# Moving the last 2 KB of every wo row onto seven chosen DMA engines by a software-issued side load

## Chip, cores, metric

One core of one Trainium2 chip. The metric is device microseconds of one execution. The profile's page counts 16 DMA engines for the core (its queue rows are shares of 16 engines' span). The kernel before takes 196.09 us (median of 3 runs, 195.96 to 196.11).

## The reference, cut to what matters

One decoding step for a batch of 4: attention of 32 query heads over the last 4096 positions of 8 key/value heads, then the output projection with `wo`, mixed with a small gated feed-forward block.

```
q = x @ wq                      # heads 32 x 128
p = softmax(q @ k.T * Dh**-0.5)  # k, v: last 4096 positions, 64 MB together
o = p @ v
a = o.reshape(B, 32 * 128) @ wo # wo is 4096 x 512 bf16: 4 MB, the last thing loaded
out = g * a + (1 - g) * ffn(x)
```

About 81 MB must come from memory once. Everything else hides behind that, except the work that follows the last bytes of `wo`.

## The kernel before: the parts in question

`Wo` is a tile of 128 partitions with 32 KB of `wo` each, cut into 64 units of 512 B per partition. It arrives in five pieces. All loads are issued by the sync engine (hardware queue), the last piece in three row blocks of 123, 3 and 2 rows.

```python
WO_PIECES = ((0, 34), (34, 52), (52, 60), (60, 63), (63, 64))   # units of 512 B
LOW3 = (0, 123, 126, 128)                                       # row blocks of the last piece
...
            elif k == "wo":
                lo, hi = WO_PIECES[it[1]]
                wo = A_wo.rearrange("(p i) c -> p (i c)", i=32)
                for n, r in enumerate(wo_rows(it[1])):           # 128 rows, or the LOW3 blocks
                    load(("WO", it[1], n), f"d_wo{it[1]}", Wo[r, OW * lo:OW * hi], wo[r, OW * lo:OW * hi], waits=w)
...
        def WO(p):                                               # tensor engine, one matmul a unit
            lo, hi = WO_PIECES[p]
            w = [("WO", p, n) for n in range(len(wo_rows(p)))] + [("E", "OQ")]
            for x in range(lo, hi):
                i, j = x // OUTT, x % OUTT
                mm(banks[ACC][OR * j:OR * j + 4, 0:OW], oq[:, i, :], Wo[:, OW * x:OW * x + OW], False, i == 31, ...)
```

Loads go out in the order wq, x, gate_w, the K and V sets, W_gate, W_up, last V, W_down, wo pieces. The slot of `wo` is free once the value product of set 6 is done, at 170.9 us.

## Time and profile before

| | before |
|---|---|
| time | 196.09 us |
| span of the profiled execution | 194.8 us |
| mean DMA rate | 416 GB/s |
| last landing of wo | 192.60 us |
| engines that land late (put down to instruction fetches below) | 6 of 16 |

The page's slice rows (40 slices of 4.9 us: busy share of the DMA engines in tenths, and GB/s) and its queue rows (packets, MB, share of 16 engines' span):

```profile
DMA  6999999999999999999999999999999999999992
GB/s 215 431 432 431 437 437 431 431 427 451 431 437 437 446 427 424 431 437 431 431 431 431 427 424 437 444 437 431 431 431 421 431 395 427 470 431 384 425 404 90
q1 hardware_dynamic: 3610, 81.01, 97.3%
q8 instruction: 5, 0.08, 0.2%
q14 instruction: 1, 0.01, 0.0%
```

From the second slice to the last but one the engines are busy 90% or more (9 tenths): the kernel is bound by its loads. The five 16 KB packets of q8, of the kind "instruction", are instruction fetches; they took 1.02 to 1.07 us each.

The end of the chain that ended last (start us, us, what):

```profile
171.74 20.41 DMA slots<-in_A_wo_dram
192.16 0.04 issue
192.20 0.87 PE bank L320 x12
193.07 0.02 issue
193.09 0.42 DVE osum L577
```

The tensor engine waits for `wo`. The twelve matmuls after 192.20 are the third piece's last eight units and the four units of the last two pieces; among them is one more wait, for the landing at 192.60.

Two stretches (window us, busy time of the engines, granted clock, DMA share, GB/s):

```profile
176.00:180.00 4.00, 1.51 (x8) 0.84 (x10) 0.00 (x0) 0.00 (x0) 0.00 (x0) 0.74 0.98 417
180.00:184.00 4.00, 4.00 (x38) 2.09 (x35) 0.00 (x0) 0.44 (x1) 0.00 (x0) 0.83 1.00 422
```

The page does not show the engines one by one. The trace does, in a way: it has sixteen landings for each of these loads, read here as one for each engine. Sorted landings (us) of the third wo piece (60 units of each row are then there), and of the fourth (63 units):

```
before, 60 units: 190.20 190.25 190.32 190.33 190.37 190.38 190.40 190.49 190.50 190.71 | 191.45 191.93 191.94 191.95 192.04 192.16
before, 63 units: 190.70 190.75 190.83 190.84 190.89 190.89 190.90 190.98 191.09 191.23 | 191.88 192.35 192.37 192.40 192.47 192.60
```

Ten engines are early, six late by 1.0 to 1.8 us, counted from the median of the ten. The gaps appear one by one, after each of the five 16 KB fetches and the one 8 KB fetch at 63.3 us (0.33 us): one late landing of sixteen after the first fetch, three after the third, six after the sixth. That a late engine is one that carried a fetch is inferred from this: no record names an engine. The unevenness is what the old last piece, and the change, try to use: give work to early engines. The three row blocks of the old last piece have eight landings together (191.87 to 192.39; three earlier updates of their semaphore, up to 184.90, precede the piece's first packet at 190.30), not sixteen each.

### The profile page before, as it was taken

Reading aid. Unit: us, or ns where it says so; the run is one execution under the profiler, and the core shown is the slowest. Engines: PE = TensorE matmul, PEld = TensorE weight load, DVE = VectorE, ACT = ScalarE, POOL = GpSimd, SP = SyncE. Lnnn points to the kernel's source line nnn. Section 1 sums busy time; section 2 is a strip of 40 time slices with the busy share of each in tenths; the row PEclk is TensorE's granted clock in tenths of the full one; section 3 lists DMA queues with packets and bytes.
Section 4 is the critical chain, followed back from the end, with each engine's and each line's share of the span. In section 5 each row is a group of like instructions: output and inputs, shape, how many; then the busy total and the mean of one; then the engine's idle time right before and its main releaser. Section 6 shows DMA issues by size and latency. Waiting matters only on the chain.

```text
span 194.8 us, 1734 instructions
## 1 busy us (share of the span) xinstructions
PE 120.6 (62%) x723; PEld 50.6 (26%) x723; DVE 124.1 (64%) x153; ACT 27.5 (14%) x34; POOL 9.5 (5%) x25
## 2 busy tenths in 40 slices
PE   0209279474943894686468943894586466743974
PEld 0003123121411341242112411341142122311562
DVE  6103769999399809980998199819981998370010
ACT  2213000040130013001300130013001300420100
POOL 7830000000000000000000000000000000000000
PEclk9999958999999797899876999697999889997899
DMA  6999999999999999999999999999999999999992
GB/s 215 431 432 431 437 437 431 431 427 451 431 437 437 446 427 424 431 437 431 431 431 431 427 424 437 444 437 431 431 431 421 431 395 427 470 431 384 425 404 90
DMA packets 3616, 81.10 MB, mean 416 GB/s; under 512 B 401, under 2 KB 666, under 8 KB 794
## 3 DMA queue, kind: packets, MB, share of 16 engines
q1 hardware_dynamic: 3610, 81.01, 97.3%
q8 instruction: 5, 0.08, 0.2%
q14 instruction: 1, 0.01, 0.0%
HBM read 81.01 MB, written 0.00 MB: 416 GB/s over the span
## 4 chain that ended last, share of the span: by engine, by line
DMA 54%; DVE 31%; PE 9%; issue 4%; SPq 0%; ACT 0%
DMA slots<-in_A_k_cache_dram 38%; DVE kt L491 21%; DMA slots<-in_A_wo_dram 10%; PE bank L320 7%; DMA xsb<-in_A_x_dram 6%; DVE sc L527 5%; DVE qblk L517 1%; PE bank L324 1%; DVE pT L542 1%; DVE rd L531 1%; SPq L256 0%; DVE negmax L537 0%; ACT gwB L600 0%; DVE osum L577 0%; DVE mx L527 0%
## 5 line engine op out<-in xcount | busy, mean ns | idle before, releaser
L491 DVE STREAM_TRANSPOSE kt<-slots 128x2048 f32<-128x2048 f32 x32 | 73.7, 2305 | 28.1 <-DMA slots<-in_A_k_cache_dram 28.0
L320 PE MATMUL bank<-kt,qblk 128*128 128x512 bf16 x256 | 72.1, 434 | 27.9 <-DVE kt L491 27.9
L320 PEld LDWEIGHTS bank<-kt,qblk 128*128 128x128 bf16 x256 | 25.2, 107 | 69.7 <-DVE kt L491 36.0
L320 PE MATMUL bank<-slots,pT 128*64 128x512 bf16 x256 | 32.3, 410 | 5.7 <-DMA slots<-in_A_v_cache_dram 5.7
L619 ACT ACTIVATE pe<-sc,negmax 128x2048 bf16<-128x2048 bf16 x8 | 16.0, 2002 | 60.1 <-DVE negmax L537 60.1
L527 DVE CUSTOM_DVE_ANT_0 sc<-bank,maskf 128x512 bf16<-128x512 f32 x32 | 21.0, 658 | 3.8 <-PE bank L320 3.7
L320 PEld LDWEIGHTS bank<-slots,pT 128*64 128x64 bf16 x256 | 15.1, 118 | 23.2 <-issue 13.4
L542 DVE STREAM_TRANSPOSE pT<-pe 128x2048 bf16<-128x2048 bf16 x8 | 18.5, 2312 | 2.2 <-ACT pe L619 2.2
L604 ACT ACTIVATE osb<-bank 128x512 bf16<-128x512 f32 x8 | 4.8, 597 | 81.5 <-PE bank L320 81.5
L320 PE MATMUL bank<-rd,grpb 128*128 128x32 bf16 x8 | 1.6, 194 | 22.1 <-DVE rd L531 22.1
L555 DVE TENSOR_TENSOR oq<-bank,recip 64x128 bf16<-64x128 f32 x2 | 0.9, 434 | 12.3 <-PE bank L320 12.2
L320 PEld LDWEIGHTS bank<-rd,grpb 128*128 128x128 bf16 x8 | 0.8, 98 | 25.7 <-DVE rd L531 25.7
L495 DVE COPY xT<-bank 128x20 bf16<-128x20 bf16 x1 | 0.2, 171 | 8.0 <-PE bank L324 8.0
L320 PE MATMUL bank<-slots,oq 128*4 128x256 bf16 x64 | 4.0, 272 | 2.0 <-DMA slots<-in_A_wo_dram 2.0
L320 PE MATMUL bank<-slots,xT 128*4 128x512 bf16 (+1 forms) x64 | 5.0, 467 | 0.0
L320 PE MATMUL bank<-maskr,maskl 128*128 128x512 bf16 x1 | 0.6, 609 | 5.9 <-POOL maskr L296 5.9
L517 DVE TENSOR_SCALAR qblk<-bank 32x64 uint32<-32x64 uint32 x16 | 2.9, 215 | 2.1 <-PE bank L324 2.1
L324 PE MATMUL bank<-identb,xsb 5*128 5x5 bf16 x4 | 0.3, 168 | 5.7 <-DMA xsb<-in_A_x_dram 5.7
L577 DVE CAST osum<-bank 4x256 bf16<-4x256 f32 x1 | 0.4, 418 | 5.2 <-PE bank L320 5.2
L320 PEld LDWEIGHTS bank<-slots,oq 128*4 128x4 bf16 x64 | 2.5, 84 | 3.5 <-DMA slots<-in_A_wo_dram 2.9
L296 POOL TENSOR_SCALAR_AFFINE_SELECT fold<-fold 128x256 bf16<-128x256 bf16 x8 | 3.3, 417 | 1.1
L486 DVE MEMSET qblk<- 128x2304 uint32 x1 | 2.0, 1978 | 1.3 <-PEq L644 1.3
(59 smaller groups left out, 40.3 us busy)
## 6 DMA issues: line engine op xcount, KB each, us to landing
slots<-in_A_k_cache_dram SPq DMA_DIRECT2D x8, 4096.0 KB, 25.1
slots<-in_A_v_cache_dram SPq DMA_DIRECT2D x8, 4096.0 KB, 30.5
slots<-in_A_wq_dram SPq DMA_DIRECT2D x1, 4096.0 KB, 12.4
slots<-in_A_wo_dram SPq DMA_DIRECT2D x1, 2176.0 KB, 17.1
slots<-in_B_W_gate_dram SPq DMA_DIRECT2D x1, 1792.0 KB, 19.7
slots<-in_B_W_up_dram SPq DMA_DIRECT2D x1, 1792.0 KB, 23.6
slots<-in_B_W_down_dram SPq DMA_DIRECT2D x1, 1792.0 KB, 18.5
slots<-in_A_wo_dram SPq DMA_DIRECT2D x1, 1152.0 KB, 19.5
```

Of the source, the lines that this page charges most:

```text
L296: op(lambda: e.affine_select(dst, src, pattern, cmp, fill, base=base, channel_multiplier=mult), ev)
L320: E.op(lambda: t.matmul(out_, lhsT, rhs, start=start, stop=stop, tile_position=pos, skip_group_check=True), ev=ev, waits=waits)
L324: E.op(lambda: t.transpose(out_, in_, idn), ev=ev, waits=waits)
L486: E.op(lambda: v.memset(qblk[:, :, :, :, :].rearrange("p s h c e -> p (s h c e)"), 0.0), ev=("QZ",))
L491: E.op(lambda: v.transpose(kt[:, f, :].bitcast(FP32), slot("k", s)[:, 4096 * f:4096 * f + 4096].bitcast(FP32)), ev=("E", "KT", s, f), waits=w)
L517: E.op(lambda dst=dst, r=r, g=g: v.tensor_scalar(dst, src[r, g, 0:B, :, :], 0, None, op0=ALU.bitwise_or), ev=("E",) + keys[1] if (q, g) == ...
L527: E.op(lambda: v.tensor_tensor_reduce(sc[:, 512 * f:512 * f + 512], banks[scb(key)], R["maskf"][:, :], 1.0, -3.0e38, ALU.add, ALU.max, mx4 ...
L531: E.op(lambda: v.tensor_tensor(rd32[:, :, :], bc(R["own8"][:, :].unsqueeze(2), 2, 4), bc(mx4[:, :].unsqueeze(1), 1, 8), ALU.mult), ev=("MA ...
L542: E.op(lambda: v.transpose(pT[:, s % 2, :], pe[:, :]), ev=("E", "PT", s), waits=[("EXP", s)] + ([("PV", s - 2)] if s >= 2 else []))
L555: E.op(lambda g=g, r=r: v.tensor_tensor(oq[r, :, :].rearrange("p i b -> p b i"), banks[tr(key)][0:64, 128 * g:128 * g + 128].rearrange("p ...
L604: E.op(lambda: a.activation(osb[:, s, :], ob(s), ACTF.Copy), ev=("NORM", s), waits=[("PV", s)])
L619: E.op(lambda: a.activation(pe[:, :], sc[:, :], ACTF.Exp, bias=negmax[:, s % 2:s % 2 + 1], scale=SCALE, accum_out=rowsum[:, s:s + 1]), ev= ...
```

## The change

Intent: let the six late engines stop at unit 60, and bring units 60 to 63 (2 KB a row) as a side load on engines that are early. 119 of its rows go out by GpSimd's software descriptors, after a tiny "turn" transfer to shift which engines they use; 9 rows go by the sync queue. The side load is issued as soon as the slot is free and multiplied first. Core of the diff:

```diff
-WO_PIECES = ((0, 34), (34, 52), (52, 60), (60, 63), (63, 64))
-LOW3 = (0, 123, 126, 128)
+WO_PIECES = ((0, 32), (32, 48), (48, 56), (56, 60))
+SIDE = (60, 64)
+SIDE_ROWS = (0, 119, 124, 128)
...
+    sb("turn", [12, 2, 8], BF16)
...
+                if it[1] == 0:
+                    for n in (1, 2):
+                        load(("SIDE", n), "d_side_hw", *side(n), waits=w)
+                load(("WO", it[1]), f"d_wo{it[1]}", Wo[:, OW * lo:OW * hi], wo_all[:, OW * lo:OW * hi], waits=w)
... (GpSimd)
+        E.op(lambda: e.dma_start(R["turn"][:, :, :], gate_w[0:384].rearrange("(p t c) -> p t c", p=12, t=2)[:, :, 0:8]), ev=("TURN",),
+             ctr="d_turn")
+        E.op(lambda: e.dma_start(*side(0), max_dma_last_dim=1024), ev=("SIDE", 0), waits=[("TURN",)] + slot_wait[("wo", 0)],
+             ctr="d_side")
... (tensor engine: WO(None), the side units, comes before WO(0))
```

More of the change, by code (lines that the diff above doesn't have):

```diff
@@ L155, in _order @@
     o += [("SC", s, 3), ("SW", s), ("PV", s - 1), ("PT", s), ("RS", 1), ("GU",), ("PV", s), ("FFN",), ("OQ",)]
-    return o + [("WO", p) for p in range(len(WO_PIECES))]
+    return o + [("WO", None)] + [("WO", p) for p in range(len(WO_PIECES))]
 def _dma_order():
@@ L240, in sc_free, with side @@
         return [("E",) + sck[n]] if n >= 0 else [("INIT",)]
-    def wo_rows(p):
-        return [slice(a, b) for a, b in zip(LOW3, LOW3[1:])] if p == len(WO_PIECES) - 1 else [slice(0, 128)]
+    wo_all = A_wo.rearrange("(p i) c -> p (i c)", i=32)
+    def side(n):
+        r, c = slice(SIDE_ROWS[n], SIDE_ROWS[n + 1]), slice(OW * SIDE[0], OW * SIDE[1])
+        return Wo[r, c], wo_all[r, c]
     def set_of(s):
@@ L275, in sync @@
                 lo, hi = WO_PIECES[it[1]]
-                wo = A_wo.rearrange("(p i) c -> p (i c)", i=32)
-                for n, r in enumerate(wo_rows(it[1])):
-                    load(("WO", it[1], n), f"d_wo{it[1]}", Wo[r, OW * lo:OW * hi], wo[r, OW * lo:OW * hi], waits=w)
+                if it[1] == 0:
+                    for n in (1, 2):
+                        load(("SIDE", n), "d_side_hw", *side(n), waits=w)
+                load(("WO", it[1]), f"d_wo{it[1]}", Wo[:, OW * lo:OW * hi], wo_all[:, OW * lo:OW * hi], waits=w)
             else:
@@ L424, in WO @@
         def WO(p):
-            lo, hi = WO_PIECES[p]
-            w = [("WO", p, n) for n in range(len(wo_rows(p)))] + [("E", "OQ")]
+            lo, hi = SIDE if p is None else WO_PIECES[p]
+            w = [("SIDE", n) for n in range(3)] + [("E", "OQ")] if p is None else [("WO", p)]
             for x in range(lo, hi):
                 i, j = x // OUTT, x % OUTT
-                mm(banks[ACC][OR * j:OR * j + 4, 0:OW], oq[:, i, :], Wo[:, OW * x:OW * x + OW], False, i == 31,
+                mm(banks[ACC][OR * j:OR * j + 4, 0:OW], oq[:, i, :], Wo[:, OW * x:OW * x + OW], False, i == WO_PIECES[-1][1] // OUTT - 1,
                    ev=("WOP", p) if x == hi - 1 else None, waits=w if x == lo else (), pos=(0, OR * j))
@@ L623, in FIN @@
             E.op(lambda: a.activation(osum[:, 0:OW], banks[ACC][0:4, 0:OW], ACTF.Copy), ev=("OSUM", 0),
-                 waits=[("WOP", len(WO_PIECES) - 2)])
+                 waits=[("WOP", len(WO_PIECES) - 1)])
         fns = dict(ECONST=ECONST, GWB=GWB, EQ=EQ, GE=GE, RELU=RELU, EXP=EXP, NORM=NORM, FIN=FIN)
```

## The prediction

> **What bounds the kernel.** The transfers. In the page's slice rows the DMA share is 9 tenths in every slice from the second to the last but one, at about 431 GB/s; PE is busy 62%, DVE 64%. In the chain of waits the last long piece is the wo load (20.41 us, to 192.16); after it come only PE x12 (0.87 us) and the final copy (0.42 us). So the time is set by when the slowest of the 16 DMA engines finishes its share.
>
> **Engines are uneven.** The trace's landings[...] of wo's first piece come in two groups: ten at 186.11 to 186.63, six at 187.23 to 188.01. The packet records explain it: five 16 KB instruction fetches (about 1.05 us each[...]) and one 8 KB fetch fell on six engines. These six stay 0.8 to 1.6 us behind. The third piece (60 of 64 units of 512 B per row) lands by 192.16, the 3-unit piece by 192.60, and the tensor engine's last four multiplications start at 192.64.[...]
>
> **What the change does.** The common part shrinks from 63 to 60 units, so every slow engine loses 8 packets of 1536 B (65 ns each in the trace): 0.52 us. The last four units become a side load: 119 rows of 2 KB in a GpSimd-issued transfer, 9 rows on the sync queue[...].[...]
>
> **Costs.** Each chosen engine gets 17 rows as 34 packets of 1 KB at about 46 ns (the x rows' packets): an estimate of 1.5 us, plus 0.1 to 0.17 us of sync-issued rows[...]. Fast engines land their 60th unit at 190.2 to 190.7, so the chosen ones should now land at 191.7 to 192.3: level with the slow ones at about 192.15. The side load can start when the slot frees (170.9); interleaved with V, W_down and wo it delays fast engines there by up to 1.5 us, which hides behind the slow ones.[...] Its four units are multiplied first, from about 188. PE keeps 54 ns per unit.
>
> **Critical path.** Last landing 192.60 -> about 192.2, then four multiplications (0.4 us), copy 0.42 us, store unchanged. Gain about 0.4 us of 196.09, 0.2%. Prediction 195.70 us, range 195.35 to 196.15. Faster by over 2%: 0.005; within 2%: 0.98; slower by over 2%: 0.015.
>
> **What would show it.** Last wo landing 192.0 to 192.3 with all 16 engines within 0.5 us; 119x2 packets of 1 KB on a second queue, finished before 188; final PE group starting at about 192.2, idle before it ended by the wo load; copy at about 192.6; V's last landing moved by under 0.2 us.
>
> **What would make it wrong.** The 119 rows go to all 16 engines, or to engines that carry the instruction fetches: then the slowest engine gains nothing or loses up to 1.5 us. Instruction fetches move to other engines. Software descriptors prove slower than the 46 ns packets[...]. V lands late enough that PE, with 0.3 us of slack, becomes the limit.

The sum: 190.2 to 190.7 plus 1.5 us, and 0.1 us or so for the sync queue's rows, is 191.7 to 192.3; the last landing then goes from 192.60 to about 192.2, and 0.4 us off 196.09 is 195.7. The cost of "turn" (put at under 0.1 us) was no term of it. The 17 rows for each chosen engine are 119 / 7, and the seven was an assumption.

## The result

| | before | after |
|---|---|---|
| time, median | 196.05 us (195.96 to 196.11, 4 runs) | 198.59 us (198.21 to 198.80, 4 runs) |
| span of the profiled execution | 194.8 us | 197.2 us |
| last landing of wo | 192.60 us | 194.98 us |
| last landing of V / W_down | 178.35 / 182.65 us | 179.25 / 186.04 us |

The ratio is 1.0128 (95%: 1.0110 to 1.0146). A ratio here is the mean time of one kernel's fast runs over the mean of the other's in the same rounds, so not quite the ratio of the medians. The change lost 2.5 us; a gain of 0.4 us was predicted.

The same page rows after:

```profile
DMA  6999999999999999999999999999999999999991
GB/s 219 439 453 445 452 439 425 425 422 425 425 425 425 420 432 429 439 445 439 445 439 425 422 425 432 432 425 425 425 425 422 435 408 441 438 397 323 388 391 61
q1 hardware_dynamic: 3492, 80.77, 96.7%
q0 software_dynamic: 192, 0.25, 0.4%
q8 instruction: 5, 0.08, 0.2%
q14 instruction: 1, 0.01, 0.0%
```

The engines are as busy as before, but one slice (177.5 to 182.4 us) moves 323 GB/s where the kernel before moved 384 in the same slice and 431 and 425 in those beside it. "Busy" is the time packets were under way; slow packets look busy. The same two windows as before show it closer:

```profile
176.00:180.00 4.00, 0.61 (x4) 0.42 (x6) 0.00 (x0) 0.00 (x0) 0.00 (x0) 0.70 1.00 321
180.00:184.00 4.00, 4.00 (x21) 1.89 (x18) 0.00 (x0) 0.00 (x0) 0.00 (x0) 0.50 1.01 332
```

Same DMA share within 0.02, a fifth to a quarter less data. The issue on GpSimd and the end of the kernel, from the timeline (start us, us, engine, line, operation, tiles):

```profile
12.29 0.72 POOL L321 DMA_DIRECT2D turn<-in_gate_w_dram  x1 [0.19 <-issue]
171.64 0.97 POOL L323 DMA_DIRECT2D slots<-in_A_wo_dram  x1 [158.63 <-PE bank L330]
```

```profile
172.51 21.84 DMA slots<-in_A_wo_dram
194.35 0.04 issue
194.40 0.60 PE bank L330 x8
195.00 0.03 issue
195.03 0.40 PE bank L330 x4
195.43 0.02 issue
195.45 0.42 DVE osum L587
```

The last lines are the end of the chain after. Its form is the predicted one, a last landing, four multiplications (0.40 us), a copy (0.42 us), but it begins at 194.98 in place of 192.2.

Two facts of the trace say where the time went. First, the packet records: the software packets ran from 176.0 (4.4 us after their issue began at 171.64) to 184.8 us, and in that time the ordinary packets of all engines took longer. Mean duration of packets that started between 176 and 182 us (a packet of 14336 B is one row of `W_down`):

```
before: 14336 B packets 539 ns            (128 packets)
after:  14336 B packets 716 ns            (106 packets), software 4096 B packets 180 ns
```

The long packets stand everywhere: before, every one of the 128 packets took less than 560 ns; after, every one of the 106 took more than 600 ns, though the side rows, by the count of their packets (56 of 4096 B, 7 of 2048 B: 8 + 1 seven times), were on seven engines only. Second, the landings of the 60th unit of each row:

```
after, 60 units: 192.24 192.25 192.27 192.28 192.47 | 193.35 193.36 193.45 193.59 193.65 193.66 193.69 193.83 194.00 | 194.89 194.98
```

Even the five earliest engines land 2.0 us later than the five earliest of before (means 192.30 and 190.29). Nine engines follow, then two, 0.9 us behind the rest. The counts fit a simple reading, which is inferred and not recorded: seven engines with software side rows and six with a fetch, two of them with both, leave five with neither. In numbers: predicted last landing 192.2; fourteen engines done at 194.00 (1.8 us more; the five earliest lost as much); last two at 194.98 (1.0 us more).

### The profile page after: what moved, and what is told of

Same layout as the page of the kernel before. It is cut to its first block, busy times and chain, and to the rows that moved or that the text cites. A ratio compares the mean times of both kernels' runs of the same rounds, so it can differ in the third digit from the quotient of the medians.

```text
span 197.2 us, 1736 instructions
## 1 busy us (share of the span) xinstructions
PE 122.8 (62%) x723; PEld 51.7 (26%) x723; DVE 124.2 (63%) x153; ACT 27.5 (14%) x34; POOL 11.2 (6%) x27
## 4 chain that ended last, share of the span: by engine, by line
DMA 54%; DVE 30%; PE 9%; issue 5%; SPq 1%; ACT 0%
DMA slots<-in_A_k_cache_dram 37%; DVE kt L501 21%; DMA slots<-in_A_wo_dram 11%; PE bank L330 8%; DMA xsb<-in_gate_w_dram 6%; DVE sc L537 5%; PE bank L334 2%; DVE qblk L527 1%; DVE pT L552 1%; SPq L261 1%; DVE rd L541 1%; DVE negmax L547 0%; ACT gwB L610 0%; DVE osum L587 0%; DVE mx L537 0%
## 5 line engine op out<-in xcount | busy, mean ns | idle before, releaser
L330 PE MATMUL bank<-kt,qblk 128*128 128x512 bf16 x256 | 73.6, 440 | 26.4 <-DVE kt L501 26.4
L330 PEld LDWEIGHTS bank<-kt,qblk 128*128 128x128 bf16 x256 | 25.7, 109 | 69.6 <-DVE kt L501 34.1
L323 POOL DMA_DIRECT2D slots<-in_A_wo_dram x1 | 1.0, 972 | 158.6 <-PE bank L330 158.6
```

Source lines behind the costliest of these rows:

```text
L323: E.op(lambda: e.dma_start(*side(0), max_dma_last_dim=1024), ev=("SIDE", 0), waits=[("TURN",)] + slot_wait[("wo", 0)], ctr="d_side")
L330: E.op(lambda: t.matmul(out_, lhsT, rhs, start=start, stop=stop, tile_position=pos, skip_group_check=True), ev=ev, waits=waits)
```

## The experiments

A ring is here a DMA queue of the profile: q0 holds the software's transfers, q1 those of the sync engine, q10 those of the scalar engine. A turn is a change from one ring to another.

Theories at the start: A, every turn between the software ring and the hardware ring costs all engines time. B, two of the seven chosen engines also carry an instruction fetch. C, the bytes of the side load slow everybody.

### e1_single: one software packet per engine

```diff
-e.dma_start(*side(0), max_dma_last_dim=1024)
+e.dma_start(*side(0), max_dma_last_dim=1024, single_packet=True)
```

> The changed kernel with the software side load packed into one packet per engine (34 descriptors) in place of nine. Theory A, each turn between the software ring and the hardware ring costs every engine about 0.18 us and lengthens the hardware packets: with one turn the W_down packets of 14336 B go back from 710 ns to about 540 ns, the five fastest engines land wo at about 190.8 in place of 192.3, and the time falls to about 197.0 us; what is left over the kernel before (about 0.9 us) is theory B, side rows on two engines that carry instruction fetches. Rival C, the 238 KB that software descriptors move[...] slow everyone: unchanged, 198.5 us and 710 ns.

Measured: 198.49 us (198.34 to 198.82), ratio 1.0123. The option did nothing: the trace has the same 56 packets of 4096 B and 7 of 2048 B. So the run tests no theory. It is a repeat of the changed kernel, and shows the same pattern: 14336 B packets 705 ns, two engines apart at the end (194.88 and 195.01, the rest by 193.59).

### e2_k16: all 128 side rows in software, on all engines

```diff
-SIDE_ROWS = (0, 119, 124, 128)    # and the turn transfer, and the two sync-issued row blocks: gone
+SIDE_ROWS = (0, 128)
```

> All 128 side rows in one software transfer over all 16 engines (8 rows, 16 descriptors, 4 packets each), no turn transfer, no sync-issued rows: no engine is chosen, so theory B cannot act, and the six slow engines do all of their 64 units. Theory A: four turns in place of nine, loss about 0.7 us; the last wo landing at about 193.4 and the time about 197.0 us. Rival C (bytes): 710 ns packets for as long as the same 256 KB take, 1.5 us or more lost, 197.8 us. If software transfers cost nothing: 196.3 us, the price of giving up the uneven last piece.

Measured: 196.62 us (196.40 to 196.88), ratio 1.0021. Most of the loss is gone (0.5 us is left), with more side bytes by software than in the changed kernel (256 KB against 238). 14336 B packets took 552 ns. So neither the bytes alone (C) nor software descriptors alone make packets 716 ns. What remains has another cause than expected, shown by the chain and a window of this run:

```profile
147.72 31.52 DMA slots<-in_A_v_cache_dram
179.24 0.14 issue
179.37 9.75 PE bank L325 x76
```

```profile
180.00:184.00 4.00, 4.00 (x21) 1.89 (x18) 0.00 (x0) 0.00 (x0) 0.00 (x0) 0.50 1.03 435
```

V landed at 179.24, 0.9 us later than before, on one engine; the tensor engine then ran its value product at a granted clock of 0.50 (0.83 before, in the same window), and from there on it was the limit, not the loads.

### e3_act: the 119 rows by the scalar engine's hardware queue

```diff
-  (GpSimd: turn, side load)
+  (scalar engine, after NORM 6) a.dma_start(*side(0))      # 119 rows
```

> The 119 side rows issued by the scalar engine's hardware queue[...], no software transfer. If any second ring beside the sync queue's slows the packets (theory A in its general form), 14336 B packets[...] rise to about 700 ns; if only software descriptors do (theory A in its narrow form), they stay at 540 ns. [...]the last landing is expected at about 193.8 and the time at 197.2 us if nothing else is lost, 198.5 us if the ring costs as much as the software one.

Measured: 198.00 us (197.63 to 198.40), ratio 1.0096. No software descriptor is left, and 14336 B packets still took 621 ns, 16384 B packets 724 ns (615 ns where undisturbed). The narrow form of A falls. One engine landed at 194.63, the other fifteen by 193.72.

### e4_small9: software turns without bytes

```diff
 (kernel before, GpSimd, at the moment of the side load)
+for n in range(9): e.dma_start(tiny[:, 2n:2n+2, :], <32 rows x 2 pieces of 16 B of wo>)
```

> The kernel before, plus nine software transfers of 32 rows x 2 pieces of 16 B to an unused tile, at the moment at which the side load was issued[...], 9 KB in all. Theory A (turns between rings, whatever they carry): 14336 B packets at about 700 ns while they last, and 1.5 us lost, 197.6 us. Rival C (bytes) : packets stay at 540 ns, 196.1 to 196.4 us.

Measured: 196.66 us (196.44 to 196.82), ratio 1.0026. Packets of 14336 B took 563 ns. Turns between the rings cost something, about 25 ns a packet (563 against 539), but not 180; its five earliest engines land the 60th unit 0.3 us later than before. So theory A explains a small part of the loss.

A new theory, P, fits all four: what makes the packets of other loads long is how the rows of a load are laid out over the partitions, not its bytes, its ring or its kind of descriptor. Beside 128 rows (e2) packets of 14336 B took 552 ns; beside the 119 rows they took 621 ns (e3) and 716 ns (the changed kernel). No trace here names an engine or a partition, so P stands as a guess about the layout that the runs can test. The next runs hold bytes, packets and ring fixed and change only the partitions.

### e5_m128, e6_m64, e7_m32: the same extra bytes to 128, 64 or 32 partitions

All three: kernel before plus an unused 256 KB load on the scalar engine's hardware queue, into a free part of a slot, 128 packets of 2 KB and 16 completions in each trace (read as 8 packets on each of 16 engines). Theory P expects no harm from the first form, whose layout is that of the large loads, and harm from the other two.

```diff
+a.dma_start(slot("wd")[0:128, 8192:9216],  <128 rows x 2 KB of wo>)       # e5
+a.dma_start(slot("wd")[0:64,  8192:10240], <the same rows, 2 a partition>) # e6
+a.dma_start(slot("wd")[0:32,  8192:12288], <the same rows, 4 a partition>) # e7
```

> The kernel before plus an unused extra load from the scalar engine's hardware queue at the moment of the side load: 256 KB as 128 rows x 2 KB, 8 packets of 2 KB on each of 16 engines[...]. New theory P:[...] 14336 B packets at most 570 ns beside the second ring, and the time rises by the bytes alone, 8 x 84 ns = 0.7 us, to about 196.9 us. Rival R, any second ring with bulk data: packets at 650 to 710 ns and 198 us.

> The same 256 KB from the same addresses in the same number of 2 KB packets per engine, but written as 2 x 2 KB to each of 64 partitions[...]. Theory P: 14336 B packets at 650 to 750 ns while it lasts, 197.6 to 198.4 us, at least 0.6 us above the 128-row form. Rival R: the same as the 128-row form.

> The same 256 KB as 4 x 2 KB to each of 32 partitions[...]. Theory P: as the 64-row form or worse, 198 us or more. Rival R: the same as the 128-row form.

Measured: 196.79 us (196.72 to 196.81), 197.93 us (197.82 to 198.50) and 198.19 us (197.88 to 198.31); ratios 1.0028, 1.0092 and 1.0098. Packets of 14336 B: 542, 687 and 657 ns. In the 128-row form they are about as short as without a second ring (539 ns), and the cost is the bytes' own 0.6 us (8 packets at 85 ns are 0.68). In the 64-row form the same bytes cost 1.1 us more, and again everywhere: every one of the 124 packets of e5 took less than 560 ns, every one of the 111 of e6 more than 600. The 32-row form is no worse than the 64-row form (the intervals of the ratios overlap). The windows of e5, then of e6:

```profile
176.00:180.00 4.00, 1.30 (x8) 0.69 (x10) 0.00 (x0) 0.00 (x0) 0.00 (x0) 0.75 0.95 394
180.00:184.00 4.00, 4.00 (x36) 2.13 (x34) 0.00 (x0) 0.29 (x1) 0.00 (x0) 0.82 1.05 438
```

```profile
176.00:180.00 4.00, 0.36 (x2) 0.22 (x4) 0.00 (x0) 0.00 (x0) 0.00 (x0) 0.77 0.95 313
180.00:184.00 4.00, 4.00 (x22) 1.97 (x20) 0.00 (x0) 0.00 (x0) 0.00 (x0) 0.50 1.03 389
```

In the first stretch the DMA share is 0.95 in both, the rate 394 against 313 GB/s. This is the after-kernel's signature without one software descriptor and without chosen engines. What it is in the layout is not separated here: the 64-row and 32-row forms crowd the bytes into fewer partitions. Crowding alone doesn't explain the changed kernel, which spreads its side rows over 119 partitions, but no run has another layout than the 128-row one without crowding and with all 16 engines.

### e8_hw: the 119 rows in the sync queue itself

```diff
-for n in (1, 2):        # rows 119 to 127
+for n in (0, 1, 2):     # all three side blocks; GpSimd's two transfers gone
```

> The changed kernel with the 119 rows as one more transfer of the sync queue[...], so that one ring holds everything and nothing takes turns. Theory P:[...] packets of the other engines at 650 ns or more for some 2 us after W_down, and the time is near that of the scalar-queue form, 197.6 to 198.2 us. If two rings are needed for the loss, packets stay at 615 ns[...]: 197.2 us or less.

Measured: 198.17 us (197.63 to 198.35), ratio 1.0090. One ring, no turns at all, and the loss is there: 14 packets of 16384 B that started before 182 us took 870 ns, the side packets that started before then 114 ns in place of 84. The window confirms it:

```profile
180.00:184.00 4.00, 3.94 (x26) 2.06 (x23) 0.00 (x0) 0.02 (x1) 0.00 (x0) 0.72 1.04 309
```

The five earliest engines land the 60th unit at 191.90 to 192.14 (mean 191.97), so 1.7 of the 2.0 us that these engines lost in the changed kernel come without software descriptors. The remaining 0.3 us are a difference of two kernels, in line with the 0.3 us of e4. Three engines ended late here (194.24 to 194.87, the others by 193.61).

### e9_six, e13_six_b, e14_six_c: six engines that were thought to be free of fetches

```diff
-SIDE_ROWS = (0, 119, 124, 128)   # software: 119 rows
+SIDE_ROWS = (0, 57, 114, 128)    # software: 57 rows; sync: 57 and 14
-sb("turn", [12, 2, 8], BF16)
+sb("turn", [4, 2, 8], BF16)
```

> The changed kernel with the side load on engines believed free of instruction fetches: 57 rows by software[...], 57 by the sync queue[...], 14 single rows[...]. Theory B: in the changed kernel two of the seven chosen engines also carried a fetch and land 1 us after the next; here no engine carries both, so the last landing is at about 193.7 to 194.0 in place of 194.98, with no separate pair at the end, and the time is about 197.5 us. If B is wrong: 198.4 us as before. Theory P[...] leaves the rest of the loss, so the time stays over 197 us.

That these rows go to six engines, and to which, was the expectation; no record shows it.

Measured: 198.47 us (197.41 to 198.88), ratio 1.0113. The profiled execution was the one of 197.41 us. Its last landing was at 193.95, and no engine stood apart, just as B expects; but the three others took 198.42 to 198.88. Two more executions of the same kernel were profiled:

> The six-engine kernel again, for the profile. Its first profiled execution took 197.41 us with the last landing at 193.95 as theory B expected, its timed ones 198.42 to 198.88 us. If instruction fetches fall on the same engines in every execution, this profile shows no engine far behind the others, last landing within 0.2 us of 193.95, and 197.4 us. If the engines of the fetches change between executions, a profile of about 198.5 us shows one or more engines about 1 us behind all others at the end, last landing near 195.

> As e13_six_b: one more execution. 197.4 us and no late engine if the fetches' engines are fixed; some executions with late engines at about 198.5 us if they are not.

Measured: profiled at 198.66 and 198.80 us. Both show two engines apart at the end:

```
e9_six    (197.41 us): ... 193.68 193.69 193.77 193.84 193.95
e13_six_b (198.66 us): ... 193.98 194.06 194.07 194.11 | 194.93 195.18
e14_six_c (198.80 us): ... 193.92 193.94 194.16 194.35 | 195.32 195.33
```

### e15_after_b: the changed kernel once more

> The changed kernel once more. If the fetches' engines are fixed: two engines about 0.9 us behind the other fourteen at the last landing, as in its first profile and in e1_single. If they vary: another count than two.

Measured: 198.59 us twice. This time one engine stood apart (195.13, the others by 194.08), not two. So how many engines stand apart changes between executions of one kernel. The profiles compared are from different chips (e9 on chip 11, e13 to e15 on chip 7), but the times of e9 alone, on one chip, differ by over 1 us. That the engines apart are those with a fetch and side rows is inferred. It fits the count and the size of the gap.

What it is that moves stays open, and a rival to the fetches was not tested: no record shows that the software's transfers go to the same engines in every execution, so the chosen engines may move while the fetches stay. The times of e3 and e8, which have no software transfer at all, spread over 0.7 to 0.8 us too, but so do those of e6 (0.7 us), which chooses no engines; so the record does not settle it.

Ratios of this call (e13 to e15) are from one or two runs each and their verdicts were unclear; one execution of the kernel before took 393.41 us there and is left out as slow.

### e10_even: no uneven piece at all

```diff
-WO_PIECES = ((0, 34), (34, 52), (52, 60), (60, 63), (63, 64))   # last one in LOW3 row blocks
+WO_PIECES = ((0, 34), (34, 52), (52, 60), (60, 64))             # all on 16 engines
```

> The kernel before with its uneven last piece taken away: wo in four pieces of 34, 18, 8 and 4 units, every one on all 16 engines, sync queue only. [...]The six slow engines carry one unit more: 8 packets, about 0.2 us: 196.3 us. The difference from the run with 128 side rows in software (196.62 us, 0.52 us over its own kernel before) is then the price of software descriptors by themselves, about 0.3 us. If the small uneven piece costs as much as it gives: 196.1 us.

Measured: 196.06 us (195.99 to 196.54, 5 runs), before 196.09 us in the same rounds; ratio 1.0004 (0.9991 to 1.0016). The end of its chain:

```profile
172.19 19.71 DMA slots<-in_A_wo_dram
191.91 0.04 issue
191.95 0.60 PE bank L320 x8
192.55 0.03 issue
192.58 0.40 PE bank L320 x4
```

The last landing is at 192.53, not later than before. So the uneven last piece that the kernel already had buys nothing measurable. The difference from e2 is not a clean price of software descriptors, because e2 ended on the tensor engine.

### e11_m128c, e12_m64c: is it the source?

```diff
+as e5 and e6, but the 256 KB are read from one contiguous block
```

> As the extra load of 128 rows x 2 KB, but read from one contiguous block of 256 KB in place of rows 32 KB apart. If theory P holds (destination partitions decide), this is as cheap: packets of 14336 B at 545 ns, 196.8 us. If the source pattern decides, it may differ.

> The same contiguous 256 KB written as 2 x 2 KB to each of 64 partitions. Theory P: packets of 14336 B at 650 to 780 ns, 197.9 us, as with the spread source. If the source pattern decides: as the contiguous 128-row form.

Measured: 196.71 us (196.62 to 196.95) and 198.19 us (197.95 to 198.34); ratios 1.0036 and 1.0106; packets of 14336 B 542 and 686 ns. In the four cells (spread or contiguous source, 128 or 64 partitions) the source makes no difference beyond the noise, and the destination does.

What stays open: why the layout matters. The runs show only that for this extra load the arrangement of partitions decides. That it is also the cause for the 119 rows of the changed kernel is inferred from the same long packets in e3 (621 ns for 14336 B) and e8 (870 ns for 16384 B); that those rows are on fewer than sixteen engines remains a rival there, since no run varied it with the layout fixed.

## Why the prediction was wrong, point by point

- **Load-bound, six late engines, last landing plus four multiplications and a copy.** Right; the chain after has that form with 0.40 and 0.42 us.
- **"Each chosen engine gets 17 rows as 34 packets of 1 KB at about 46 ns ... the chosen ones should now land at 191.7 to 192.3: level with the slow ones at about 192.15."** This step failed. It priced a side row by the time of the engine that carries it, and took everyone else's packets as unchanged. The runs showed the reverse: while those rows were under way, 14336 B packets went from 539 to 716 ns, and engines without side rows lost 2.0 us each. Rows that follow the usual 128-partition layout do not do this (542 ns in e5), the same rows to 64 partitions do (687 ns in e6), with no software in either. The price for the engine that carries them was right: they came as nine packets an engine, not 34, and these took 1.55 us together, against 1.5 predicted. What was missing from the sum is the price for the other engines.
- **Which engines carry the side rows**. The seven-way split is in the trace: 56 + 7 packets are 8 + 1 on each of seven engines, and 72 packets of 16 B and 9 of 8 B in the same queue fit 8 + 1 on each of the nine others. The numbers of the engines are in no record. But the hope for a set of engines that stays free of fetches seems to have failed (inferred, as above): two engines were apart in the first profile (1.0 us), two in e1, one in e15, and for a set of six none, two, two. The prediction listed both engines with fetches and fetches that move as risks, but kept them out of its number and its range.
- **"V's last landing moved by under 0.2 us".** Wrong: 0.90 us (178.35 to 179.25). The delay of the early engines did not hide behind the late ones, because the late ones were slowed too (the latest landed W_down at 186.04 in place of 182.65).
- **"Finished before 188" and "a second queue"**: right (landed by 185.87). **PE as a new limit**: it delayed the first matmuls of wo (190.79, after the attention output `oq` of the vector engine, not after a landing) but caught up; the last wait is for wo.
- **Sum.** Last landing predicted 192.2, measured 194.98: 1.8 us that the others lose too (most of it put down to the rows' layout, about 0.3 us estimated for software turns from e4 and e8) and 1.0 us from two engines apart, read as engines with both burdens.

No version beat the kernel before; the plain even cut (e10) ties with it and is simpler.

## What to carry to other kernels

When all DMA engines are busy, moving bytes from one engine to another was not free here: a load of 256 KB in the ordinary 128-row layout cost its own bytes (0.6 us, e5), in 64 partitions 1.1 us more (e6), with packets of other loads at 687 in place of 542 ns. Try the 128-row layout first, or count the slowdown of the others. Test such a load first as an unused extra transfer and look at the durations of the other packets; the busy share does not show it (0.95 in e5 and in e6, at 394 and 313 GB/s). And before choosing engines by name, profile the same kernel several times, because how many end late may change (none, two and two of e9's kernel in three profiles).
